# Sliding-window attention with sink tokens, then a gated feed-forward block: one sink table built later, sink scores of two groups in one run, crossbar transposes issued at earlier places

## The chip, the cores and the metric

The kernel runs on one core of a Trainium2 chip. Five engines work side by side on a core: TensorE (PE in the profile, with its weight loads as PEld), VectorE (DVE), ScalarE (ACT), GpSimd (POOL) and SyncE (SP), the last used here only to start DMAs. They synchronise through semaphores. TensorE reads SBUF and writes PSUM; PSUM has eight banks, and this kernel hands all of them out from one pool. The metric is device microseconds of one execution; lower is better.

## The reference, cut to what matters

```python
def _attn_ref(q, k, v, n_sink, window):          # batch 4, heads 8, seq 768, head_dim 64
    scores = (1 / sqrt(D)) * q @ k.T
    keep = (pos_k < 4) | ((0 <= pos_q - pos_k) & (pos_q - pos_k < 128))
    scores = where(keep, scores, -1e9)
    a = softmax(scores)
    return a @ v

x = attn_out.transpose(0, 2, 1, 3).reshape(3072, 512)
def _moe_ref(x, w_gate, w_val, w_out):           # 512 -> 1536 -> 512
    g = x @ w_gate
    return (g * sigmoid(g) * (x @ w_val)) @ w_out
```

Each query sees the four sink keys and the 128 keys of its window. The maximum is not subtracted in the kernel, and a column of ones beside V gives the sum of each row.

## The kernel before, in words

**Groups.** The 3072 tokens are cut into 12 groups of 256 tokens, three to a batch: group `g` is part `c = g % 3` of batch `b = g // 3`. A group passes these steps, each with its own function:

- Load (`load4`, `load1`, `load_v`, and `next_load(g)`, which loads group `g+4`): keys, queries and values by DMAs that POOL starts. The keys and queries of a group lie in a tile `kq` (four buffers).
- Transposition of keys and queries: groups 0 to 3 on TensorE (`step_T`, tile `pt`, copied to `kT` and `qT` by ACT and DVE); groups 4 to 11 by the DMA crossbar (`cross_T`, line 304, tile `kqT`, four buffers), two DMAs that SP starts. `C(g)` is `cross_T(g)` followed by `next_load(g)`; for `g` of 8 and above there is nothing left to load.
- `step_S(g, p2)`: window scores of four heads into four PSUM banks (line 334), the exponential by ACT (`e`, line 341), and a multiplication by the band mask by DVE (line 346), which is put on a list `later`.
- `step_K(g)`: sink scores of the group against the four sink keys of its batch, four matmuls into a bank `pk` (line 357) and the exponential `es` by ACT (line 361). Groups with `c == 0` need none, because for them the window mask takes in the sinks.
- `step_PV(g, j, hh)`: for 128 queries and four heads, probabilities times values into a bank `o` (line 381); the first matmul takes `es` and the sink value table `vsb` of the batch. DVE (`rcp` line 386, `xn` line 393; ACT in a few places, line 389) normalises. `vsb` (128 x 520) is made by POOL from a small fp32 table `vcf` and a diagonal pattern (`build_vsb`, line 188), once per batch.
- The normalised rows are transposed once more into `xT`: on TensorE (`step_X`, line 417) for groups 0 to 2 and 4, by the DMA crossbar from SP (line 399) for group 3 and from group 5 on.

**Feed-forward.** The tokens of `xT` are taken in eight blocks of 256, 256, 256, 512, 512, 512, 512 and 256. For a block, `gate(tb, f, attn)` computes a bank of the gate projection `pg` (line 445), lets ACT take its tanh (`th`, line 452), runs the attention steps of its slot, computes the value projection `pv` (line 445), and lets DVE form the product in two instructions (`u` line 459, `ht` line 460); then it empties `later`. `down(tb, ts, attn)` multiplies by `w_out` (`pd`, line 498), ACT copies (`ot`, line 502), and SP starts the store (line 504). The gate and value weights come in five chunks of two, two, two, two and four columns of 128 (`load_gate(0)` to `load_gate(4)`), by POOL's DMAs.

**The order is written by hand.** There is no scheduler: each engine executes what the Python code emits, in that order. `weave(units, slots)` runs through a list of `gate` and `down` calls and emits in each the attention steps of that slot. In a `gate`, they stand between `pg` and `pv`. There is a prologue (groups 0 and 1 up to the first scores), a first weave of 25 units (blocks 0 to 2 beside groups 1 to 4), three weaves of 16 units (block 3 with groups 5 and 6, block 4 with 7 and 8, block 5 with 9 and 10), and a last one (blocks 6 and 7 with group 11). The function `pair(ga, gb, sh)` gives the slots of two groups; `sh` shifts them. A sink-score run stands by itself in the second score slot of its group:

```python
        return [((s, s + 2), Ss(ga)), (s + 2, [K(ga)]),
                ...
                ((s + 6, s + 8), Ss(gb)), (s + 8, [K(gb)]),
```

**Queues.** The DMA queues of SP and POOL work in order as well: a DMA that waits holds up those behind it. Each starter's DMAs take eight semaphores in turn, so one also waits until the DMA eight places earlier has landed. A PSUM bank is handed out in the order in which earlier tiles were given back, so a step more or less shifts which earlier tile a later step waits for. In the prologue, POOL's order is: values of group 0, group 1, weight chunk 0, the two patterns for the table, values of group 1, chunk 1, `build_vsb(0)`, chunks 2 to 4.

Of the kernel before, what the change touches and what calls it, by code (L numbers as in the profile page):

```python
# [8 lines left out]
FP32 = mybir.dt.float32  # L9
BF16 = mybir.dt.bfloat16  # L10
AF = mybir.ActivationFunctionType
# [4 lines left out]
def kernel(  # L16
# [12 lines left out]
    nc = tc.nc  # L29
    P = 128  # L30
# [9 lines left out]
    NP2 = H // 2  # L40
# [12 lines left out]
    scale = 1.0 / float(D) ** 0.5  # L53

    def pool(name, bufs, psum=False):
        if psum:
            return ctx.enter_context(
                tc.tile_pool(name=name, bufs=bufs, space=bass.MemoryType.PSUM))
        return ctx.enter_context(tc.tile_pool(name=name, bufs=bufs))
# [8 lines left out]
    espool = pool("espool", 2)  # L68
# [11 lines left out]
    def bank(shape, dtype, name):  # L80
        return psum.tile(shape, dtype, tag="b", name=name)
# [36 lines left out]
    def load_v(g):  # L118
        va = new_v(g)
        b, c = divmod(g, GC)  # L120
        for j in range(2):
            t0 = c * 256 + j * P
            nc.gpsimd.dma_start(  # L123
                va[:, j, :, 0:D], v[b, :, t0:t0 + P].rearrange("h m d -> m h d"))
# [3 lines left out]
    def load_gate(i):  # L128
        f0, n = sum(FCH[:i]) * P, FCH[i] * P
        for lst, w, nm in ((wgs, moe_w_gate, "wg"), (wvs, moe_w_val, "wv")):  # L130
            t = wpool.tile([P, DMC, n], BF16, tag=f"{nm}{i}", name=nm)
            nc.gpsimd.dma_start(
                t, w[:, f0:f0 + n].rearrange("(c p) f -> p c f", p=P))
            lst.append(t)
# [17 lines left out]
    vsbs, kss = [], []  # L152
    KS = 32
# [32 lines left out]
    def build_vsb(b):  # L186
        vsb = const.tile([P, H, D + 1], BF16, tag=f"vsb{b}", name="vsb")
        nc.gpsimd.tensor_tensor(
            vsb,
            vcf[:, b:b + 1].broadcast_to([P, H, D + 1]),  # L190
            diag_h.rearrange("q (h o) -> q h o", o=1).broadcast_to([P, H, D + 1]),
            op=ALU.mult)
        vsbs.append(vsb)
# [19 lines left out]
        pattern=[[32, NP2], [NS, 2]], channel_multiplier=-1)  # L213
    load_v(1)
    load_gate(1)
    build_vsb(0)
    for i in range(2, 5):
        load_gate(i)

    def build_masks():  # L220
# [12 lines left out]
    kTs, qTs, es_t, e_t, xns, xTs = {}, {}, {}, {}, {}, {}  # L233
    later = []

    def A(fn, *a):
        return lambda: fn(*a)
# [12 lines left out]
    def step_T(g, ph, q_late=False, q_act=False):  # L250

        if ph == 0:
            new_kq(g)
        own = lambda i, p: nat[g][:, 2 * p:2 * p + 2]
        transpose(g, ph, own, (ident, ident), q_late, q_act)
# [36 lines left out]
    def queries(g, r, p, j, n):  # L292

        if g < NPE:
            return qTs[g][r, p, j * P:(j + n) * P]
        return cross[g][r, j:j + n, 1, p]
# [3 lines left out]
    def cross_T(g):  # L300

        t = crossp.tile([P, 2, 2, NP2, P], BF16, tag="kqT", name="kqT")
        for j in range(2):
            nc.sync.dma_start(
                t[:, j].rearrange("q i a m -> q (i a) m"),
                nat[g][:, j].rearrange("p i x -> p (i x)"), transpose=True)
        cross[g] = t
# [40 lines left out]
            later.append(dve)  # L348

    def step_K(g):  # L350
        b, c = divmod(g, GC)
        if c == 0:
            return
        ps = bank([P, 256], FP32, "pk")
        for p in range(NP2):

            nc.tensor.matmul(
                ps[KS * p:KS * (p + 1)], kss[b][:, p * KS:(p + 1) * KS],
                queries(g, slice(0, P), p, 0, 2), start=True, stop=True)
        es_t[g] = espool.tile([P, 256], BF16, tag="es", name="es")  # L360
        nc.scalar.activation(es_t[g], ps, AF.Exp, scale=scale)  # L361

    def step_PV(g, j, hh, act=False):
        b, c = divmod(g, GC)
# [146 lines left out]
    def gates(tb):  # L511
        return [(gate, tb, f) for f in range(0, DFC, 512 // SIZES[tb])]

    def downs(tb):
        return [(down, tb, t) for t in range(SIZES[tb] // P)]

    def next_load(g):
        if g + 4 < NG:
            (load4 if g + 4 < NPE else load1)(g + 4)
            load_v(g + 4)  # L520

    def sinks(b):
        return [lambda: later.append(A(step_ks, b))]

    def T(g):
        def last():
            step_T(g, 1)
            next_load(g)
        return [A(step_T, g, 0), last]

    def Ss(g):
        return [A(step_S, g, p2) for p2 in range(2)]

    def PVs(g):

        return [A(step_PV, g, j, hh) for hh in range(2) for j in range(2)]
# [4 lines left out]
    def K(g):  # L541
        return A(step_K, g)
# [5 lines left out]
    def weave(us, slots):  # L548
        assert all(i < len(us) for i in slots)
        for i, (fn, tb, x) in enumerate(us):  # L550
            fn(tb, x, slots.get(i, []))
# [7 lines left out]
    def slots(*pairs):  # L559
        sl = {}  # L560
        for at, steps in pairs:
            for i, step in zip(at if isinstance(at, tuple) else (at,) * len(steps),
                               steps):
                sl.setdefault(i, []).append(step)
        return sl

    def C(g):

        def last():
            cross_T(g)  # L570
            next_load(g)
        return [last]
# [41 lines left out]
    def first_PVs():  # L614
# [10 lines left out]
    weave(us, slots(  # L625
        (0, [flush, A(step_S, 1, 1), K(1), A(next_load, 1)]), (2, [first_PVs]),
        (3, [A(step_X, 1, 0), A(step_X, 1, 1, True), flush]),
        (9, T(2)), ((10, 11), Ss(2)), (11, [K(2)]),
        (12, PVs(2)[:2] + [flush]), (13, PVs(2)[2:] + [flush]), (13, C(4)),
        (14, [A(step_X, 2, 0), A(step_X, 2, 1, True), flush]),  # L630
        (15, T(3)), ((16, 17), Ss(3)), (17, sinks(1)), ((18, 18, 19, 19), PVs(3)),
# [2 lines left out]

    def pair(ga, gb, sh=0):
        s = sh
        return [((s, s + 2), Ss(ga)), (s + 2, [K(ga)]),
                ((s + 4, s + 5, s + 6, s + 7), PVs(ga)),
                ((s + 6, s + 8), Ss(gb)), (s + 8, [K(gb)]),
                ((11, 11, 12, 12) if s else (10, 11, 12, 13), PVs(gb))]  # L640

    weave(gates(3) + downs(3), slots(
        *pair(5, 6, 2), (2, C(6)), (10, C(7))))
    weave(gates(4) + downs(4), slots((0, sinks(2)), *pair(7, 8), (3, C(8)), (10, C(9)), (14, C(10))))
    weave(gates(5) + downs(5), slots((0, sinks(3)), *pair(9, 10), (10, C(11))))
    weave(gates(6) + gates(7) + downs(6) + downs(7), slots(
        ((0, 2), Ss(11)), (2, [K(11)]), ((4, 5, 6, 7), PVs(11))))


# [33 lines left out]
```

## Time and profile before

| | us |
|---|---|
| median of 6 runs | 245.44 (245.07 to 246.27) |
| the profiled execution, its own time | 245.09 |
| its span, first to last instruction | 243.4 |
| PE busy in the span | 233.9 (96%) |
| DVE busy | 160.5 (66%) |
| ACT busy | 111.3 (46%) |
| POOL busy | 71.1 (29%) |
| mean granted TensorE clock | 0.991 |

Instructions of one engine follow each other in time, and their durations can overlap at the ends, because the next one starts while the last one drains. A number in square brackets at the end of a row of the timeline is the idle time of the engine ahead of that row, with the instruction that ended it. The row of granted clock gives tenths of the full TensorE clock in 40 equal slices of the span, some 6.1 us each. TensorE is the engine with the least idle time, so the places where it stands still, and those where its clock is lowered, are what is read first.

### The profile page before, as it was taken

Reading aid. Unit: us, or ns where it says so; the run is one execution under the profiler, and the core shown is the slowest. Engines: PE = TensorE matmul, PEld = TensorE weight load, DVE = VectorE, ACT = ScalarE, POOL = GpSimd, SP = SyncE. Lnnn points to the kernel's source line nnn. Section 1 sums busy time; section 2 is a strip of 40 time slices with the busy share of each in tenths; the row PEclk is TensorE's granted clock in tenths of the full one; section 3 lists DMA queues with packets and bytes.
Section 4 is the critical chain, followed back from the end, with each engine's and each line's share of the span. In section 5 each row is a group of like instructions: output and inputs, shape, how many; then the busy total and the mean of one; then the engine's idle time right before and its main releaser. Section 6 shows DMA issues by size and latency. Waiting matters only on the chain.

```text
span 243.4 us, 5190 instructions
## 1 busy us (share of the span) xinstructions
PE 233.9 (96%) x2073; PEld 136.2 (56%) x2073; DVE 160.5 (66%) x336; ACT 111.3 (46%) x221; POOL 71.1 (29%) x92
## 2 busy tenths in 40 slices
PE   7779999999999999999999999999999999999994
PEld 2567887767755445554455454445454445488443
DVE  2688778929983489890598980399970489877100
ACT  2628627447461274532566512556612562232111
POOL 8995396794276714308000000000000000000000
PEclk9979999999999999999999999999999999999999
DMA  7999999999999999959940335900524200200132
GB/s 138 151 179 197 204 190 204 165 151 172 164 146 162 206 179 116 133 109 136 221 77 1 72 61 142 164 0 1 81 51 129 89 0 0 46 0 3 46 126 88
DMA packets 98792, 27.37 MB, mean 112 GB/s; under 512 B 84816, under 2 KB 95824, under 8 KB 98768
## 3 DMA queue, kind: packets, MB, share of 16 engines
q0 software_dynamic: 68832, 13.90, 69.8%
q1 hardware_dynamic: 29504, 12.75, 26.0%
q10 hardware_dynamic: 432, 0.39, 0.5%
q8 instruction: 16, 0.26, 0.5%
q14 instruction: 8, 0.07, 0.1%
HBM read 28.34 MB, written 6.29 MB: 142 GB/s over the span
## 4 chain that ended last, share of the span: by engine, by line
PE 87%; ACT 5%; DVE 5%; DMA 1%; issue 1%; DVEq 0%; ACTq 0%
PE pv L445 25%; PE pd L498 25%; PE pg L445 23%; PE o L381 5%; PE s L334 3%; ACT e L341 3%; PE pt L270 3%; DVE e L346 2%; PE wm L248 2%; DVE ht L460 1%; PE px L417 1%; DMA out_dram<-ot 1%; ACT xn L389 1%; DVE u L459 1%; ACT kT L275 0%
## 5 line engine op out<-in xcount | busy, mean ns | idle before, releaser
L445 PE MATMUL pv<-xT,wv 128*128 128x256 bf16 (+1 forms) x384 | 74.3, 326 | 0.9 <-DVE ht L460 0.9
L445 PE MATMUL pg<-xT,wg 128*128 128x256 bf16 (+1 forms) x384 | 74.2, 326 | 0.0
L452 ACT ACTIVATE th<-pg 128x512 f32<-128x512 f32 x72 | 43.7, 606 | 60.0 <-PE pg L445 59.4
L459 DVE SCALAR_TENSOR_TENSOR u<-th,pg 128x512 bf16<-128x512 f32 x72 | 49.2, 683 | 30.6 <-ACT th L452 30.1
L498 PE MATMUL pd<-wo,ht 128*128 128x512 bf16 x276 | 63.5, 379 | 0.0
L460 DVE TENSOR_TENSOR ht<-u,pv 128x512 bf16<-128x512 bf16 x72 | 49.5, 688 | 9.5 <-PE pv L445 2.9
L445 PEld LDWEIGHTS <-wg 128*128 128x128 bf16 x384 | 37.4, 98 | 25.4 <-issue 0.2
L341 ACT ACTIVATE e<-s 128x512 bf16<-128x512 f32 (+1 forms) x96 | 46.1, 580 | 0.9 <-PE s L334 0.8
L445 PEld LDWEIGHTS <-wv 128*128 128x128 bf16 x384 | 34.5, 98 | 21.0 <-issue 2.9
L498 PEld LDWEIGHTS <-ht 128*128 128x128 bf16 x276 | 25.8, 98 | 28.0 <-issue 0.2
L502 ACT ACTIVATE ot<-pd 128x512 f32<-128x512 f32 x23 | 13.7, 597 | 53.5 <-PE pd L498 53.5
L346 DVE TENSOR_TENSOR e<-e,mask 128x1024 bf16<-128x1024 bf16 (+1 forms) x48 | 30.4, 671 | 1.2 <-ACT e L341 1.0
L123 POOL DMA_DIRECT2D va<-in_v_dram x24 | 21.3, 896 | 5.8 <-DMA kq<-in_q_dram 2.0
L393 DVE TENSOR_TENSOR xn<-o,rcp 128x256 bf16<-128x256 f32 x46 | 19.5, 425 | 2.9 <-DMA xT<-xn 1.3
L107 POOL DMA_DIRECT2D kq<-in_k_dram x16 | 14.2, 889 | 24.1 <-DMA kqT<-kq 19.8
L381 PEld LDWEIGHTS <-e 128*128 128x128 bf16 x352 | 16.6, 99 | 7.9 <-DVE e L346 2.5
L381 PE MATMUL o<-va,e 128*128 128x65 bf16 x352 | 18.2, 195 | 2.1 <-DVE e L346 2.1
L107 POOL DMA_DIRECT2D kq<-in_q_dram x16 | 14.2, 890 | 7.1 <-DMA va<-in_v_dram 2.6
L386 DVE RECIPROCAL rcp<-o 128x4 f32<-128x4 f32 x48 | 8.4, 176 | 7.2 <-PE o L381 7.1
L275 DVE CAST qT<-pt 128x512 bf16<-128x512 f32 x7 | 4.6, 688 | 9.3 <-PE pt L270 9.3
L483 DVE TENSOR_SCALAR ot<-pd 128x256 f32<-128x256 f32 x1 | 0.4, 425 | 14.4 <-DMA out_dram<-ot 14.4
L381 PE MATMUL o<-vsb,es 128*128 128x260 bf16 x32 | 8.8, 275 | 0.7 <-ACT es L361 0.7
(61 smaller groups left out, 109.2 us busy)
## 6 DMA issues: line engine op xcount, KB each, us to landing
out_dram<-ot SPq DMA_DIRECT2D x23, 256.0 KB
va<-in_v_dram POOLq DMA_DIRECT2D x24, 128.0 KB, 9.1
kq<-in_k_dram POOLq DMA_DIRECT2D x18, 128.0 KB, 8.9
kq<-in_q_dram POOLq DMA_DIRECT2D x16, 128.0 KB, 9.1
wo<-in_moe_w_out_dram POOLq DMA_DIRECT2D x4, 384.0 KB, 12.8
wg<-in_moe_w_gate_dram POOLq DMA_DIRECT2D x4, 256.0 KB, 7.8
wv<-in_moe_w_val_dram POOLq DMA_DIRECT2D x4, 256.0 KB, 8.5
kq<-in_k_dram POOLq DMA_DIRECT2D x3, 256.0 KB, 9.6
```

Source lines behind the costliest of these rows:

```text
L107: nc.gpsimd.dma_start(x[:, j, i].rearrange("p (h d) -> p h d", d=D), src[b, :, t0:t0 + P].rearrange("h m d -> m h d"))
L123: nc.gpsimd.dma_start(va[:, j, :, 0:D], v[b, :, t0:t0 + P].rearrange("h m d -> m h d"))
L341: nc.scalar.activation(e_t[g][:, h0 + h, lo:512], pss[2 * pp + h][:, lo:512], AF.Exp, scale=scale)
L346: nc.vector.tensor_tensor(e, e, m[:, :, lo:512].broadcast_to([P, 2, 512 - lo]), op=ALU.mult)
L381: nc.tensor.matmul(o, l, r, start=(i == 0), stop=(i == len(mms) - 1), skip_group_check=True)
L393: nc.vector.tensor_tensor(xns[g, j][:, 256 * hh:256 * (hh + 1)].rearrange("p (h d) -> p h d", h=4), po[:, :, 0:D], rcp.broadcast_to([P, 4, ...
L445: nc.tensor.matmul(ps[:, i * n:(i + 1) * n], ws[fi][:, c, fo * P:(fo + 1) * P], x[:, 0:n // P, c], start=(c == 0), stop=(c == DMC - 1))
L452: nc.scalar.activation(th, pg, AF.Tanh, scale=0.5)
L459: nc.vector.scalar_tensor_tensor(u, th, 1.0, pg, op0=ALU.add, op1=ALU.mult)
L460: nc.vector.tensor_tensor(hts[tb][:, f:f + two].rearrange("p a n -> p (a n)"), u, pv, op=ALU.mult)
L498: nc.tensor.matmul(po, hts[tb][:, f, ts * P:(ts + 1) * P], wos[f // n][:, f % n], start=(f == 0), stop=(f == DFC - 1))
L502: nc.scalar.activation(ot, po, AF.Copy, scale=0.5)
```

## The change

Three things are changed; the arithmetic is the same.

1. In the prologue, `build_vsb(0)` moves behind the loads of weight chunk 2 on POOL.
2. `step_K` can take two groups in one run: for batches 2 and 3 the sink scores of parts 1 and 2 go into the two halves of one bank, and one ACT instruction (128 x 512 in place of two of 128 x 256) takes their exponential. The calls for groups 8 and 11 go. The others stand at new places: `K(2)` in slot 10 of the first weave (was 11), `K(5)` ahead of the scores of its group in slot 2 (was behind, in slot 4), `K(7)` for groups 7 and 8 in slot 2, `K(10)` for groups 10 and 11 in slot 6 of its weave (was 8).
3. The crossbar work is emitted sooner: `C(7)` in slot 6 of the weave of block 3 (was 10), `C(8)` in slot 9 of that weave (was slot 3 of the next), `C(9)`, `C(10)` and `C(11)` in slots 3, 7 and 10 of the weave of block 4 (were slots 10 and 14 of that weave and slot 10 of the next).

```diff
     load_gate(1)
+    load_gate(2)
     build_vsb(0)
-    for i in range(2, 5):
+    for i in range(3, 5):
         load_gate(i)
...
     def step_K(g):
         b, c = divmod(g, GC)
-        if c == 0:
-            return
-        ps = bank([P, 256], FP32, "pk")
-        for p in range(NP2):
-            nc.tensor.matmul(
-                ps[KS * p:KS * (p + 1)], kss[b][:, p * KS:(p + 1) * KS],
-                queries(g, slice(0, P), p, 0, 2), start=True, stop=True)
-        es_t[g] = espool.tile([P, 256], BF16, tag="es", name="es")
-        nc.scalar.activation(es_t[g], ps, AF.Exp, scale=scale)
+        n = 2 if b > 1 else 1
+        assert n == 1 or c == 1
+        ps = bank([P, n, 256], FP32, "pk")
+        for i in range(n):
+            for p in range(NP2):
+                nc.tensor.matmul(
+                    ps[KS * p:KS * (p + 1), i], kss[b][:, p * KS:(p + 1) * KS],
+                    queries(g + i, slice(0, P), p, 0, 2), start=True, stop=True)
+        es = espool.tile([P, 2, 256], BF16, tag="es", name="es")
+        nc.scalar.activation(es[:, 0:n], ps, AF.Exp, scale=scale)
+        for i in range(n):
+            es_t[g + i] = es[:, i]
...
-        (9, T(2)), ((10, 11), Ss(2)), (11, [K(2)]),
+        (9, T(2)), ((10, 11), Ss(2)), (10, [K(2)]),
...
-        return [((s, s + 2), Ss(ga)), (s + 2, [K(ga)]),
-                ((s + 4, s + 5, s + 6, s + 7), PVs(ga)),
-                ((s + 6, s + 8), Ss(gb)), (s + 8, [K(gb)]),
+        return [((s, s + 2), Ss(ga)), ((s + 4, s + 5, s + 6, s + 7), PVs(ga)),
+                ((s + 6, s + 8), Ss(gb)),
                 ((11, 11, 12, 12) if s else (10, 11, 12, 13), PVs(gb))]
     weave(gates(3) + downs(3), slots(
-        *pair(5, 6, 2), (2, C(6)), (10, C(7))))
-    weave(gates(4) + downs(4), slots((0, sinks(2)), *pair(7, 8), (3, C(8)), (10, C(9)), (14, C(10))))
-    weave(gates(5) + downs(5), slots((0, sinks(3)), *pair(9, 10), (10, C(11))))
+        (2, [K(5)]), *pair(5, 6, 2), (2, C(6)), (6, C(7)), (9, C(8))))
+    weave(gates(4) + downs(4), slots(
+        (0, sinks(2)), *pair(7, 8), (2, [K(7)]), (3, C(9)), (7, C(10)), (10, C(11))))
+    weave(gates(5) + downs(5), slots(
+        (0, sinks(3)), *pair(9, 10), (6, [K(10)])))
     weave(gates(6) + gates(7) + downs(6) + downs(7), slots(
-        ((0, 2), Ss(11)), (2, [K(11)]), ((4, 5, 6, 7), PVs(11))))
+        ((0, 2), Ss(11)), ((4, 5, 6, 7), PVs(11))))
```

## The prediction, made before the changed kernel was run

> **What bounds the kernel now.** I read first the busy shares and the granted clock, then the waits of TensorE, then the timeline around each of them.
>
> ```profile
> PE 233.9 (96%) x2073; PEld 136.2 (56%) x2073; DVE 160.5 (66%) x336; ACT 111.3 (46%) x221; POOL 71.1 (29%) x92
> PEclk9979999999999999999999999999999999999999
> ```
>
> TensorE is the bound. It is idle for 243.4 - 233.9 = 9.5 us, and its clock is low in one place after the start, the third slice. A change can gain there, or by less TensorE work. The waits (total, times, longest):
>
> ```profile
> PE o L381 <- DVE e L346: 2.1, 3, 1.1
> PE pv L445 <- DVE ht L460: 0.9, 3, 0.4
> PE o L381 <- ACT es L361: 0.7, 2, 0.4
> ```
>
> The first is the prologue. Rows of the timeline (start, us, engine, instruction) of DVE, POOL and TensorE:
>
> ```profile
> 9.83 0.56 DVE L346 TENSOR_TENSOR e<-e,mask 128x768 bf16<-128x768 bf16 x1
> 10.60 0.56 DVE L346 TENSOR_TENSOR e<-e,mask 128x768 bf16<-128x768 bf16 x1 [0.21 <-ACT e L341]
> 11.36 1.12 DVE L346 TENSOR_TENSOR e<-e,mask 128x768 bf16<-128x768 bf16 x1 [0.21 <-ACT e L341]
> 12.41 1.41 DVE L346 TENSOR_TENSOR e<-e,mask 128x768 bf16<-128x768 bf16 x1
> ...
> 12.12 1.29 POOL L188 TENSOR_TENSOR vsb<-vcf,diag_h 128x520 bf16<-128x520 f32 x1
> ...
> 13.88 0.73 PE L381 MATMUL o<-va,e 128*128 128x65 bf16 x10 [1.10 <-DVE e L346]
> ```
>
> Four equal mask multiplications: two take 0.56 us, the two that overlap POOL's table build take 1.12 and 1.41, and TensorE stands still for the last one. The clock follows (columns: PE, PEld, DVE, ACT, POOL busy, clock):
>
> ```profile
> 10.49:13.90 3.41, 1.26 (x17) 0.69 (x16) 3.09 (x4) 1.61 (x5) 3.41 (x5) 1.00 1.35 173
> 13.90:17.32 3.42, 3.42 (x82) 2.96 (x82) 2.83 (x10) 1.07 (x2) 3.25 (x5) 0.50 1.93 175
> ```
>
> After 3.4 us in which TensorE was busy for only 1.26, it runs 3.4 us at half clock. The chain of waits shows that this stretch sets the end:
>
> ```profile
> 13.88 0.73 PE o L381 x10
> 14.61 1.00 PE pt L270 x30
> 15.61 0.97 PE px L417 x8
> 16.58 1.00 PE pt L270 x32
> 17.57 0.57 ACT kT L275
> ```
>
> The three later places where the sink scores stand in the way:
>
> ```profile
> 45.00 0.28 PE L381 MATMUL o<-vsb,es 128*128 128x260 bf16 x1 [0.35 <-ACT es L361]
> ...
> 135.59 0.29 PE L357 MATMUL pk<-kqT,ks 128*32 128x256 bf16 x4
> 136.09 1.02 PE L445 MATMUL pv<-xT,wv 128*128 128x512 bf16 x4 [0.21 <-DVE ht L460]
> ...
> 171.70 0.29 PE L357 MATMUL pk<-kqT,ks 128*32 128x256 bf16 x4
> 172.31 1.02 PE L445 MATMUL pv<-xT,wv 128*128 128x512 bf16 x4 [0.32 <-DVE ht L460]
> ```
>
> **Part 1, the table behind chunk 2.** POOL ends the issue of chunk 1 at 12.14. Two issues of chunk 2 follow (0.81 and 0.76 in the rows at 13.36 and 14.16), and the table starts at about 13.7. Each issue also waits until the DMA eight places earlier has landed: keys and queries of group 1, issued at 5.32 and 6.00, 6.1 and 6.7 us to landing, hence 11.4 and 12.7: in time for 12.12 and 12.9. From chunk 3 on POOL's order is as before. The table is read first at 22.90, so 15.0 in place of 13.4 costs nothing.
>
> Masks: they start 0.77 apart (9.83, 10.60, 11.36), so the fourth can start at 12.13 and, at 0.56, end at 12.69 in place of 13.82: 1.13 earlier. The third is stretched although the table's row begins only at 12.12, when it should have been done (11.92). POOL's spans are rough, but if something else stretches it, the gain is 0.85 (12.41 + 0.56 = 12.97). Descriptor work is no candidate: the first two ran beside DMA issues (9.76, 10.62) at 0.56.
>
> [...]
>
> What is late next is DVE's normalisation, four pairs of `rcp` and `xn`. The last ended at 16.02, 2.20 after the mask; that becomes 14.89. The table now lies beside these (13.7 to 15.0). Bounds: nothing, by `u` and `ht` of 0.69 beside the builds at 31.43 to 34.53, whose other rows are 0.69 too; or up to the 1.41 that both masks lost. I take nothing: `u`, `ht` and `xn` each have one input in PSUM, both mask inputs are in SBUF.
>
> After the last `xn` come four `px` and 32 `pt`: 17.57 - 16.02 = 1.55 at half clock. At full clock, four `px` take 0.23 (50.54 to 50.77) and 32 `pt` 0.51 (half of the 1.02 for 64 at 36.76), with 0.05 to start 0.79. So ACT's copy at 17.57 comes 1.13 earlier at half clock, 1.13 + 0.76 = 1.89 at full clock. Which? In the 3.41 us to 13.90, TensorE would be busy 1.26 plus about 0.9 of scores and transposes, 63%. The stretch before (7.08 to 10.49) had 2.65, 78%, and kept the clock; 37% lost it. 63% is nearer to 78%: full clock, and 1.1 stays an end.
>
> [...]
>
> Cover for the 1.89: chunk 1 lands at 10.62 + 7.8 = 18.4 and 11.36 + 8.4 = 19.8; TensorE would want it at 18.7 and 19.6. The 0.2 lies under the wait for ACT's `es` (22.90, now 21.0). Queries of group 2 land at 20.07 + 14.1 = 34.2; wanted at 36.69 - 1.89 = 34.8, a margin of 0.6. From there to 100 us the DMA engines are full, and loads keep their own times.
>
> **Part 2, the sink scores.** `K(2)` sooner: ACT's `es` is done before the scores of slot 11. The first `o` waited until 45.00, `pg` before it started at 43.62 and takes 0.87 in a row: 44.49 is possible, gain 0.51. Late next is ACT: `th` of slot 11 moves from 42.07 to 42.5, `u` from 43.00 to 43.1, the last mask from 45.71 to 45.84, wanted at 46.5: covered.
>
> Slots 8 of the weaves of blocks 4 and 5: `pk` takes 0.23, then `pv` waits for a bank. Without `pk` in the slot, `pv` takes the bank that `pk` took, freed by `u` (134.56 + 0.68 = 135.24) and not by the `ht` after it (136.04). It starts at 135.59, 0.50 earlier; in block 5 likewise 0.61. The four matmuls of `K(8)` and `K(11)` are done elsewhere, behind four others: 0.11 more (256 columns, as in `pv` 128x256, 0.87 for 8) to 0.23 (a run alone). Block 4: 0.50 - 0.23 + (0.23 - 0.11 to 0.23) = 0.27 to 0.39. Block 5: 0.61 - 0.23 = 0.38 to 0.50; the pair in slot 6 needs a bank that `ht` frees at 167.02 and `pv` one that `xn` frees at 167.56, and they want them at 167.35 and 167.7: covered, barely. ACT: one instruction of 0.61 for two of 0.44, off the path; behind it in slot 6 `th` ends at 170.4, before DVE asks for it at 170.79. The pairs need `kqT` of groups 8 and 11 sooner, at 122 and 167; they are issued at about 102 and 139. `K(5)` ahead of its scores: same work, `kqT` landed by 79.6 (its load buffer was reused then). I take 0.51 + 0.3 + 0.4 = 1.2, with ends 0 and 1.4.
>
> **Part 3, crossbar work.** SP does not wait for slots, only for its queue and for data. Transposes of group 7 follow those of group 6 at 87.8 (82.08 + 5.69) in place of 105.14, group 8 comes at 102, groups 9 to 11 at 118, 134 and 139. With `C(7)` goes the last load, group 11: six issues of 0.89, last in POOL's queue, from 110.18 to about 100. Behind the moved pairs on SP wait `xT` of groups 5, 7 and 8, 2.6 us for a pair (105.14, 137.98); wanted at 116.67 and 153.91, due at 104.8, 138 and 148. Off the path: nothing, between the bounds of the slow rival and zero.
>
> **The sum.** 1.89 + 1.2 = 3.1. The profiled execution took 245.09 (span 243.4, 1.7 around it): 242.0. The median lies 0.35 above that execution: 242.4 for the median after.
>
> **The rivals.** (a) The half clock stays: 1.13 + 1.2, 242.8 by the execution, 243.1 by the median. For it: 63% is untested. (b) The masks stay stretched, because the table is not the cause: 1.2 alone, 243.9 to 244.2. Against it: the two stretched rows are the two that touch the build. (c) The gain is given back to loads that keep their own times, at 34.2 and later: under 0.7 in all. Against it: the margins above. (d) Slower: the pair of group 7, now issued while the DMA engines are full, holds up the pair of group 6 in front of it. That one landed by 94.52 (POOL's wait) and is wanted by the scores at 98.19 - 3 = 95.2. If it is pushed back by the time of a pair, up to 7.83 in SP's rows, TensorE waits to 102.4, 7.2 us: 245.4 - 3.0 + 7.2 = 249.6. It turns the sign from a landing after 98.9 on. Against it: the queue serves the pair in front first.
>
> **How the numbers follow.** A measurement of this kernel tells 0.3%, 0.74 us, from no change. Forecast 0.50, (a) 0.27, (b) 0.09, (c) 0.06, (d) 0.08. The first three are faster by more: 0.86. Range: below, 1.4 in part 2 and 0.35 of spread, 241.7; above, to the end of (b), 244.2. Left out are (c) and (d), 0.14.
>
> **What would show it.** Right: all four masks at 0.56; no 1.10 wait ahead of `o`; no 0.50 clock after the start-up; `es` and both `ht` waits gone, the one of 0.41 at 66.75 still there, some 2.4 to 3 us earlier; scores of group 6 without a wait. Wrong: a mask over 1 us, `xn` over 0.43 beside the table, a wait for a DMA ahead of `pt` or `s`.

## The result, and the profile after

| | us |
|---|---|
| median before | 244.99 (72 runs, 243.14 to 246.44) |
| median after | 244.67 (35 runs, 243.71 to 246.67) |
| ratio after / before | 0.9996, 95% interval 0.9982 to 1.0009 |
| span of the profiled execution, before and after | 243.4, 242.9 |

No change that this measurement can tell. The forecast was 3.1 us less (242.4, from the median of 245.44 that six runs gave; 72 runs give 244.99), so the question is where they went. The page after has the same shape as the page before, TensorE busy a little less and the low clock still in the third slice:

```profile
PE 233.0 (96%) x2073; PEld 135.0 (56%) x2073; DVE 159.2 (66%) x336; ACT 110.9 (46%) x219; POOL 70.7 (29%) x92
PEclk9979999999999999999999999999999999999999
```

The waits of TensorE after the change (total, times, longest). Both waits for `es` and two of the three for `ht` are gone, as forecast. At the top stands a wait that the kernel before does not have; "issue" means that the profile names no releaser. The 0.8 us of `pt` lies at 7.04, at the keys of group 0 and ahead of everything that was changed:

```profile
PE pg L450 <- issue: 1.7, 1, 1.7
PE o L386 <- DVE e L347: 1.4, 3, 0.5
PE pt L271 <- DMA kq<-in_k_dram: 0.8, 1, 0.8
PE pv L450 <- DVE ht L465: 0.4, 1, 0.4
```

The start-up, in rows of the timeline of DVE and POOL. The four masks are equal now, and the table (last row) is built behind them:

```profile
9.62 0.56 DVE L347 TENSOR_TENSOR e<-e,mask 128x768 bf16<-128x768 bf16 x1 [0.66 <-ACT e L342]
10.39 0.56 DVE L347 TENSOR_TENSOR e<-e,mask 128x768 bf16<-128x768 bf16 x1 [0.21 <-ACT e L342]
11.15 0.56 DVE L347 TENSOR_TENSOR e<-e,mask 128x768 bf16<-128x768 bf16 x1 [0.21 <-ACT e L342]
11.92 0.56 DVE L347 TENSOR_TENSOR e<-e,mask 128x768 bf16<-128x768 bf16 x1 [0.21 <-ACT e L342]
...
13.47 1.13 POOL L188 TENSOR_TENSOR vsb<-vcf,diag_h 128x520 bf16<-128x520 f32 x1
```

From the first mask to the end of the fourth it is 12.48 - 9.62 = 2.86 us, before it was 13.82 - 9.83 = 3.99: the 1.13 of the forecast, to the hundredth. The clock did not follow (columns as before: PE, PEld, DVE, ACT, POOL busy, clock):

```profile
7.78:11.20 3.42, 2.70 (x48) 1.47 (x41) 2.31 (x7) 2.98 (x8) 3.33 (x6) 1.00 1.46 173
11.20:14.61 3.41, 2.18 (x60) 1.45 (x56) 3.07 (x11) 1.67 (x4) 3.41 (x6) 1.00 1.62 182
14.61:18.02 3.41, 3.29 (x51) 2.30 (x52) 2.17 (x10) 1.95 (x5) 2.92 (x4) 0.50 1.75 184
```

TensorE was busy for 2.18 of 3.41 us, 64%, and the next 3.4 us ran at half clock all the same. These stretches begin at 7.78 and 11.20 here, and at 7.08 and 10.49 before: they do not start with the program.

Where the rest went is read by laying the two chains of waits side by side and comparing the start of the same piece of work. Before:

```profile
36.76 1.02 PE pt L270 x64
...
98.70 0.97 PE pv L445 x4
...
119.22 0.86 PE pg L445 x4
...
224.44 12.96 PE pd L498 x60
```

After:

```profile
35.72 1.02 PE pt L271 x64
...
97.14 0.97 PE pv L450 x4
...
99.45 7.94 DMA xT<-xn
...
108.53 7.48 DMA xT<-xn
116.01 1.00 issue
117.01 1.02 PE pg L450 x4
...
119.55 0.86 PE pg L450 x4
...
223.91 12.96 PE pd L503 x60
```

TensorE is 1.04 us ahead at the transposes of group 2, 1.56 at 98.70, 0.33 behind at the second `pg` of block 4, and 0.53 ahead at the last projection. So 1.89 us are lost in one place, the start of block 4, whose first `pg` waits for the normalised rows that the crossbar transposes, and 0.86 are won after it. That the page names no releaser ("issue") hides a DMA: the last of the four pieces of `xT` landed at 116.81, and `pg` began 0.20 later, at 117.01. In `after_no_table` below, where the profile does name the DMA, it is 0.20 too (117.31 and 117.51).

The slots where `pk` stood in the way, after the change; `pv` follows the scores with no wait ahead of it:

```profile
135.49 0.61 PE L335 MATMUL s<-kqT 64*128 64x128 bf16 x12
136.04 1.04 PE L450 MATMUL pv<-xT,wv 128*128 128x512 bf16 x4
...
171.45 0.62 PE L335 MATMUL s<-kqT 64*128 64x128 bf16 x12
171.99 1.04 PE L450 MATMUL pv<-xT,wv 128*128 128x512 bf16 x4
```

### The profile page after: what moved, and what is told of

It is laid out like the page before. It is cut to its first block, busy times and chain, and to the rows that moved or that the text cites. A ratio compares the mean times of both kernels' runs of the same rounds, so it can differ in the third digit from the quotient of the medians.

```text
span 242.9 us, 5187 instructions
## 1 busy us (share of the span) xinstructions
PE 233.0 (96%) x2073; PEld 135.0 (56%) x2073; DVE 159.2 (66%) x336; ACT 110.9 (46%) x219; POOL 70.7 (29%) x92
## 4 chain that ended last, share of the span: by engine, by line
PE 83%; DMA 9%; ACT 2%; DVE 2%; issue 1%; POOL 0%; POOLq 0%; ACTq 0%; DVEq 0%
PE pv L450 26%; PE pg L450 25%; PE pd L503 20%; DMA xT<-xn 6%; PE o L386 5%; PE s L335 5%; DMA kq<-in_k_dram 2%; PE pt L271 2%; ACT e L342 1%; DVE xn L398 1%; DMA out_dram<-ot 1%; ACT xn L394 1%; PE pk L360 1%; PE px L422 1%; DVE rcp L391 0%
## 5 line engine op out<-in xcount | busy, mean ns | idle before, releaser
L347 DVE TENSOR_TENSOR e<-e,mask 128x1024 bf16<-128x1024 bf16 (+1 forms) x48 | 29.1, 642 | 2.1 <-ACT e L342 1.9
L335 PE MATMUL s<-kqT 64*128 64x128 bf16 (+1 forms) x168 | 9.4, 238 | 0.0
(61 smaller groups left out, 104.8 us busy)
## 6 DMA issues: line engine op xcount, KB each, us to landing
wo<-in_moe_w_out_dram POOLq DMA_DIRECT2D x4, 384.0 KB, 12.8
```

The lines of the kernel that those rows point to most:

```text
L335: nc.tensor.matmul(pss[2 * pp + h][:, col:col + n * P], keys(b, t, r, p), queries(g, r, p, j, n), start=True, stop=True)
L347: nc.vector.tensor_tensor(e, e, m[:, :, lo:512].broadcast_to([P, 2, 512 - lo]), op=ALU.mult)
```

## The experiments

SP's queue is what the experiments turn on. A group's keys and queries are one pair of crossbar transposes, its normalised rows two more. I call each DMA a piece, 5a, 5b, 6a and 6b the four pieces of rows that block 4 waits for. In the kernel before, SP issued 5a, 5b, pair 7, 6a, 6b; in the changed one pair 7, 5a, pair 8, 5b, 6a, 6b, and the load of group 11, which needs the buffer that pair 7 frees, is issued from 99.24 in place of 110.18, beside all of them. Landings are the last completion of each DMA in the trace; "wanted" is when TensorE is done with what stands ahead of the first `pg` of block 4. Behind "Measured" stand the median, that of the kernel before in the same round where it is given, and the ratio of the two kernels with its 95% interval; the ratio need not be that of the medians.

| kernel | pair 8 ahead of 5b | load of group 11 | 5a | 5b | 6a | 6b | wanted |
|---|---|---|---|---|---|---|---|
| before | no | late | 104.30 | 106.24 | 111.62 | 115.11 | 116.83 |
| changed | yes | early | 107.39 | 114.30 | 116.01 | 116.81 | 115.28 |
| `c8_behind` | no | early | 107.43 | 110.36 | 113.51 | 114.00 | 115.52 |
| `both_late` | no | late | 103.33 | 104.02 | 109.40 | 113.35 | 114.6 |
| `c8_then_c7` | yes, and pair 7 ahead of 6a | from 107 on | 104.13 | 107.17 | 115.50 | 117.23 | 115.51 |
| `no_load11` | yes | none | 105.85 | 108.89 | 109.61 | 110.90 | 114.8 |

The first piece, 5a, needs a remark. In the five traces in which SP issues pair 7 ahead of it, it took 6.9 to 7.9 us from issue to landing, and in the six others 3.0 to 4.6. The kernel without the load of group 11 is among the five (98.99 to 105.85), so the delay of 5a is for the most part not that load's. `c8_behind` and `both_late` differ in the place of `C(7)` alone: 7.74 against 4.55. With pair 7 in front, the load of group 10 landed later too: issued from 93.2 on in `no_load11` and from 93.3 in `both_late`, its last DMA landed at 106.92 and 102.75. What the load of group 11 and the pair of group 8 do shows behind 5a, from there to 6b.

### The table alone

The kernel before with one part of the change:

```diff
     load_gate(1)
+    load_gate(2)
     build_vsb(0)
-    for i in range(2, 5):
+    for i in range(3, 5):
         load_gate(i)
```

> The kernel before with the first sink table behind chunk 2 and nothing else. In the trace of the changed kernel TensorE is 1.04 us ahead at the transposes of group 2 (35.72 against 36.76), and gives everything back at 117.01, where the first gate projection of block 4 waits for the transposed rows of group 6 (landed 116.81). Queue theory: that landing was late because of the crossbar pairs and the load that were moved in front of it; without the moves it lands at 115.1 or sooner, wanted at 116.83 - 1.04 = 115.79, so the whole 1.04 stays: about 244.0 us, ratio 0.996. Floor theory: these rows land at 115 to 117 whatever comes before, since the loads keep the DMA engines full: 0.0 to 0.7 us, ratio 0.997 to 1.000. Both: all four masks of 0.56 us; the half-clock stretch of 3.4 us may shift but stays.

Measured: 243.63 against 244.98, ratio 0.9949 (0.9930 to 0.9968). The first `pg` of block 4 starts 1.43 us sooner than before (115.40 against 116.83) and the end is 1.46 us sooner by the span: what the start-up brings (1.43 here, 1.04 in the trace of the changed kernel) stays, to the end. 6b landed at 113.80. The queue theory holds, the floor theory falls.

### The table and the place of `K(2)`, nothing moved on SP

```diff
-        (9, T(2)), ((10, 11), Ss(2)), (11, [K(2)]),
+        (9, T(2)), ((10, 11), Ss(2)), (10, [K(2)]),
```

> The kernel before with the table behind chunk 2 and the sink scores of group 2 in slot 10; no merged sink scores, no moved crossbar work. TensorE should be 1.04 + 0.52 = 1.56 us ahead at 100 us, as in the changed kernel. Queue theory: the rows of group 6 land by 115.1 or sooner and are wanted at 115.27: all 1.56 stay, about 243.4 us, ratio 0.9936. Floor theory: they land at 116 or later: 0.6 us at most, ratio 0.9975 or more.

Measured: 243.30, ratio 0.9945 (0.9920 to 0.9970). In the trace TensorE is 1.69 us ahead of before at block 4 (115.14 against 116.83), no wait there (6b landed at 113.26), and 1.7 at the end. Between blocks 1 and 2 it gains 0.52: `K(2)`, as in the changed kernel. (`K(5)` was left where it was.)

### The pair of group 8 behind the rows

The changed kernel with one number changed:

```diff
-        (2, [K(5)]), *pair(5, 6, 2), (2, C(6)), (6, C(7)), (9, C(8))))
+        (2, [K(5)]), *pair(5, 6, 2), (2, C(6)), (6, C(7)), (12, C(8))))
```

> The changed kernel with the crossbar pair of group 8 in slot 12 (was 9) of the weave of block 3, which puts it behind the rows of groups 5 and 6 on SP; the load of group 11 still starts early. Queue theory, pair in front: in the changed kernel the pair of group 8 took from 107.39 to 112.88; without it the rows of group 6 land at about 111.4, wanted at 115.27: 1.56 + 0.23 (block 4) + 0.48 (blocks 5 and 6) = 2.27 us less than before, ratio 0.991. Load theory: the early load of group 11, which competes until 117.6, is what slows the rows; they land at 115 or later and 0.5 to 1.7 of the 2.27 is lost. Floor theory: nothing gained, ratio 0.999.

Measured: 242.43 against 244.98, ratio 0.9904 (0.9874 to 0.9935): 2.4 us less, with a change of one slot. SP now issues the four pieces in a row, with the pair behind them (rows of the timeline of SP):

```profile
99.69 11.33 SPq L404 DMA_TRANSPOSE xT<-xn  x4
111.12 3.10 SPq L305 DMA_TRANSPOSE kqT<-kq  x2
```

and block 4 starts without a wait (timeline of TensorE):

```profile
113.63 1.89 PE L503 MATMUL pd<-wo,ht 128*128 128x512 bf16 x8
115.36 1.03 PE L450 MATMUL pg<-xT,wg 128*128 128x512 bf16 x4
```

The rows landed at 114.00, later than the 111.4 of "pair in front" and sooner than the 115 of the load theory: with the load early and the pair of group 8 behind them the rows are in time. That 5a still lands at 107.43 is not due to that pair and, as said above, for the most part not to the load.

### Both moved back

```diff
-        (2, [K(5)]), *pair(5, 6, 2), (2, C(6)), (6, C(7)), (9, C(8))))
+        (2, [K(5)]), *pair(5, 6, 2), (2, C(6)), (10, C(7)), (12, C(8))))
```

> The changed kernel with the crossbar pair of group 7 and the load of group 11 behind it back in slot 10, and that of group 8 in slot 12: on SP the order of before, with the pair of group 8 ahead of four stores. Queue and load theory: the rows of group 6 land as before, 115.1 or up to 1.5 sooner, wanted at 115.27: the 1.56 stays, with 0.23 in block 4 and 0.48 in blocks 5 and 6 it is 2.0 to 2.3 us, ratio 0.991 to 0.992. Floor theory: landing 116 or later, at most 1.3 us, ratio 0.995 or more.

Measured: 242.42, ratio 0.9906 (0.9879 to 0.9933). No different from `c8_behind`, although the rows land 0.65 us sooner: once they are in time, more of it brings nothing. The pair of group 8 lands late here, at 120.42, and the `pk` that reads it takes 0.70 in place of 0.40 us. In this trace the clock never dropped in the start-up (1.00 in every stretch up to 23.60).

### Without the table

The changed kernel with `build_vsb(0)` back ahead of `load_gate(2)`.

> The changed kernel with the first sink table in its old place, ahead of chunk 2: only the sink scores and the crossbar work are changed. Queue theory: the rows of group 6 land when the SP queue lets them, near 116.8, and not when TensorE is done with them; so what the table brings before that is lost anyway, and without it block 4 starts at about 117 too: within 0.4 us of the changed kernel, ratio 0.998 to 1.002 against before. Additive theory: the table is worth its 1.0 to 1.4 us here as it is alone, so the time is 245.7 to 246.1, ratio 1.003 to 1.005.

Measured: 244.90, ratio 1.0005 (0.9979 to 1.0030); the changed kernel has 0.9996. The part that is worth 0.5% alone is worth 0.1% here, where the rows of group 6 are late, and the intervals do not tell that from nothing. The masks are stretched again (two in one row of DVE), and block 4 starts at 117.51 after a wait that the profile names this time:

```profile
10.88 2.79 DVE L346 TENSOR_TENSOR e<-e,mask 128x768 bf16<-128x768 bf16 x2 [0.21 <-ACT e L341]
...
117.51 1.02 PE L449 MATMUL pg<-xT,wg 128*128 128x512 bf16 x4 [1.40 <-DMA xT<-xn]
```

### Pairs in front, load behind them

```diff
-        (2, [K(5)]), *pair(5, 6, 2), (2, C(6)), (6, C(7)), (9, C(8))))
+        (2, [K(5)]), *pair(5, 6, 2), (2, C(6)), (9, C(8)), (10, C(7))))
```

> The changed kernel with the pair of group 7, and the load of group 11 that follows it, back in slot 10, while the pair of group 8 stays in slot 9: both pairs now stand in front of the rows of group 6 on SP, but the load of group 11 starts only after them. Theory that the pairs in front are enough: two pairs and three halves at 1.2 to 3 us each behind 102 put the landing at 116 or later: ratio 0.996 to 1.000. Theory that it takes the early load too (in the changed kernel the first half of the rows of group 5 needed 7.9 us beside it): the pairs move at the rate of before, 1.1 to 2.1 us a piece, the rows of group 6 land by 115.3: ratio 0.990 to 0.993.

Measured: 244.32, ratio 0.9980 (0.9957 to 1.0002), inside the range of the first expectation. The trace agrees: 6b landed at 117.23, and

```profile
117.43 1.02 PE L450 MATMUL pg<-xT,wg 128*128 128x512 bf16 x4 [1.92 <-issue]
```

By itself it does not separate the pairs from the load, since the load did not wait for pair 7 as I had expected: with the calls exchanged it takes the buffer that pair 8 frees, and POOL issues it from 107.16. Up to there SP's pieces land 0.6 to 1.4 us apart (104.13, 105.17, 106.59, 107.17), behind it 2.0, 3.6, 2.8 and 1.7. Beside `both_late` it says more: there the load starts at nearly the same time (107.92), the pair of group 8 stands behind the rows, and 6b lands at 113.35, 3.88 us sooner.

### No load at all

```diff
     def next_load(g):
-        if g + 4 < NG:
+        if g + 4 == NG - 1:
+            nat[g + 4], vas[g + 4] = nat[g + 3], vas[g + 3]
+        elif g + 4 < NG:
```

> The changed kernel without the six loads of group 11; its steps read the tiles of group 10 instead. Both crossbar pairs stay where the change put them, in front of the rows of groups 5 and 6. So far: with load and pair in front the rows of group 6 landed at 116.8 (changed kernel) and 117.2 (pair of group 7 behind that of group 8), with the load alone at 114.0. Theory that it takes the load and the pair: without the load a piece takes 1.0 to 1.4 us, as it did in front of the load in the kernel with the pairs exchanged, the rows land by 111 or as soon as TensorE and VectorE have made them, wanted at about 115.3: 1.0 to 1.7 from the start-up, 0.52, 0.38 and 0.48: ratio 0.988 to 0.992. Theory that the pair in front is enough: the rows land at 115.5 or later, ratio 0.995 or more.

The kernel leaves out the six loads of group 11, and the steps of that group read the tiles of group 10, so what it computes for those 256 tokens is not what the reference asks for. Measured: 242.28 against 244.78, ratio 0.9898 (0.9864 to 0.9932). SP's order is that of the changed kernel, and the rows land at 110.90. From 5a to 6b there are five pieces: 110.90 - 105.85 = 5.05 us here, 116.81 - 107.39 = 9.42 in the changed kernel. So neither of the two alone makes the rows late (114.00 with the load and without the pair ahead, 110.90 with the pair and without the load); together they do.

### Matmuls in the waits of the start-up

The kernel before, with warm-up matmuls of unused result put into two waits:

```diff
-    warm(2)
+    wps = warm(2)
...
-    step_PV(0, 0, 1)
+    fill(wps, 3)
+    step_PV(0, 0, 1, fills=(wps, 4))
...
```

`fill(wps, 3)` emits three of them; with `fills`, `step_PV` emits four behind its second matmul.

> The kernel before with seven matmuls of the warm-up kind (0.21 us each, their result unused) in two waits for the mask, three ahead of the third and four inside the last pair of probabilities times values. Nothing else moves, the masks stay stretched. Clock theory: a stretch of 3.41 us in which TensorE is busy for less than about two thirds is followed by one at half clock; with 1.5 us more the stretch stays above that, no half clock after the start-up, 0.5 to 0.8 us less, ratio 0.997 to 0.998. Theory that the clock drop costs nothing beside the waits: ratio 1.000.

Measured: 244.29 against 245.10, ratio 0.9975 (0.9951 to 0.9999). In the trace the masks are stretched as before, the stretch around the waits is busy for 2.93 of 3.41 us, 86%, and the next one keeps its clock:

```profile
11.21:14.62 3.41, 2.93 (x58) 1.45 (x55) 3.34 (x7) 0.58 (x2) 3.40 (x5) 1.00 1.54 181
14.62:18.03 3.41, 2.88 (x64) 1.98 (x60) 2.98 (x13) 2.40 (x5) 2.54 (x4) 1.00 1.80 182
```

TensorE is 0.85 us ahead from there to the end. All 12 timed executions kept the full clock (mean 0.997 to 1.000). The clock alone has a price, 0.85 us in this trace, near the 0.76 that the prediction gave it.

### Everything together

`c8_behind` with two, one, two and one such matmuls in the waits for the masks and ahead of `step_X(0, 0)`.

> The changed kernel with the pair of group 8 in slot 12, and six such matmuls in the waits for the masks and for the normalised rows of group 0 (two, one, two and one). Clock theory: no half clock after the start-up wherever the 3.41 us stretches fall; 0.3 to 0.9 us less than the same kernel without them (242.43): 241.5 to 242.1, ratio 0.986 to 0.989. Other theory: the time goes into the loads of group 1, wanted at 13 us, and the matmuls bring nothing: 242.4, ratio 0.990.

Measured: 242.08 against 245.10, ratio 0.9888 (0.9860 to 0.9916). The timed step from `c8_behind` is within the intervals; the traces show it. The page:

```profile
PE 232.1 (97%) x2065; PEld 134.2 (56%) x2079; DVE 159.0 (66%) x336; ACT 110.9 (46%) x219; POOL 70.8 (29%) x92
PEclk9999999999999999999999999999999999999999
```

No half clock after the start-up, span 240.3. TensorE is ahead of before by 1.77 at the transposes of group 2, 2.29 at block 4, 2.66 at block 5 and 3.15 at block 7. This is the sum that was forecast, 3.1, in the kernel that has no late rows and no low clock; its median is the lowest here, and all six timed executions kept the full clock (1.000).

## Why the prediction was wrong

**The masks (1.13): right.** 2.86 us for four in place of 3.99. All three traces with the table in its old place stretch the last two masks (1.12 and 1.41 before; 2.79 and 2.49 for the two in `after_no_table` and `before_fill`), none of the others does. The third mask is stretched although POOL's row begins after its normal end (12.12 against 11.92), so that rival (b) falls, and the 0.85 with it. `xn` beside the table kept 0.42, as assumed; that its input in PSUM is the reason was not tested. `before` and `table_only` differ by the place of the table alone (third and fourth mask 1.12 and 1.41 against 0.56 and 0.56), so the cause is shown, though not how the table stretches a mask. One cover was not costed: group 1's keys and queries, which TensorE now wants at 12.8 to 13.1. In `c8_behind` it waited 1.02 us for the queries, and its start-up gained only 0.80.

**The clock (0.76): the size of the step was right, the choice was wrong.** "63% is nearer to 78%: full clock." The share was 64%, and the clock fell. In the profiled execution rival (a), at 0.27, had this right. Two things were missing. First, the stretches were taken to begin where they did in the one profile (7.08, 10.49). In the seven traces with the table behind chunk 2 and no added matmuls they begin elsewhere each time, the first boundary after 6 us at 6.54 to 8.99 in place of 7.08; in two of them the clock stayed (`both_late`, `no_load11`: gain 1.75 and 1.73 at block 1), in five it fell (0.80 to 1.43). Second, the limit lies between the two shares that the prediction compared. `both_late`, which kept its clock, and `c8_then_c7`, which lost it:

```profile
9.95:13.36 3.41, 2.24 (x51) 1.43 (x49) 2.72 (x8) 2.13 (x6) 3.41 (x5) 1.00 1.40 186
13.36:16.78 3.42, 2.90 (x89) 2.06 (x78) 3.10 (x10) 2.04 (x4) 3.10 (x5) 1.00 1.93 175
```

```profile
11.74:15.15 3.41, 2.23 (x60) 1.51 (x64) 3.02 (x12) 1.32 (x3) 2.86 (x4) 1.00 1.68 173
15.15:18.56 3.41, 3.41 (x52) 2.30 (x49) 2.26 (x8) 2.48 (x5) 2.21 (x3) 0.50 1.65 188
```

Once the clock was up, all stretches of 2.23 us and less in the start-up of the eleven traces were followed by half clock, all of 2.24 and more by full clock: near two thirds, by a busy time that is itself modelled. This limit holds for the start-up alone. At the wait of block 4 TensorE was busy for 1.68 us (49%) of the stretch from 113.60 in the changed kernel and for 1.49 (44%) of the one from 114.14 in `c8_then_c7`, and both were followed by full clock. The matmuls there have 512 columns, those of the stretch that lost the clock in the changed kernel (11.20 to 14.61) at most 128; whether that is the reason was not tested, so a share of busy time alone does not tell when the clock falls.

**The sink scores (1.2): right.** `K(2)` 0.52, forecast 0.51. Block 4 gains 2.66 - 2.29 = 0.37 in `c8_fill` (0.27 to 0.39), blocks 5 and 6 another 3.15 - 2.66 = 0.49 (0.38 to 0.50), and the changed kernel has the same: 0.33 behind at block 4, 0.53 ahead at the end. The sum is 1.38, within the ends. (The lower end of the whole range, 241.7, comes out at 241.8 from the terms that it names: 245.44 - 1.89 - 1.4 - 0.35.)

**The crossbar work ("off the path: nothing"): wrong, and this is the step that failed.** It cost 1.89 us and undid most of the rest. The paragraph named the rows of groups 5, 7 and 8 as what waits behind the moved pairs, and left out those of group 6, which come next on the same queue, although the trace of before had them: landed 115.11, wanted 116.83. A margin of 1.72 had to bear a gain of 2.4 ahead of it and two added pieces in front; in the changed kernel they landed at 116.81, wanted at 115.28. The second error is the price: "2.6 us for a pair" came from rows of SP in which no POOL load was under way, and the same edit puts the load of group 11 beside it. Rows of group 5 "due at 104.8" landed at 107.39 and 114.30. From 5a to 6b the five pieces took 9.42 us beside the load and 5.05 without; 5a itself was late without the load too (105.85), behind pair 7.

The runs show that SP's pieces stretch beside POOL's load (five of them 9.42 us against 5.05); by what mechanism, they do not show.

**The rivals.** (c), the gain given back to transfers, at 0.06 and "under 0.7 in all", was the right kind: it named loads that keep their own times, and the late transfer was one that the change itself had made late. (d) had the right kind of cause, moved pairs among full DMA engines (the row DMA of the changed kernel's page is 9, 90% and more, from 6 to 121 us) that delay another transfer, at the wrong transfer: it held the pair of group 6 back behind that of group 7, but that one landed at 93.09 (before: 93.97), and what was held back were the rows behind.

## What to carry to other kernels

When transfers are issued sooner on a queue whose transfers land in the order of issue, as SP's did (107.39, 112.88 for the end of pair 8, 114.30, 116.01, 116.81 in the changed kernel), list every transfer that now stands behind them up to the next one with slack, with its landing and the time at which it is wanted after the gains ahead of it, and take its duration from rows with the same company. The gain ahead of the late transfer was lost whole here (1.56 us ahead at 98.70, 0.33 behind in block 4), so look for the smallest margin downstream: it capped the sum, and parts worth 1.04 and 0.52 showed nothing in the time of the changed kernel until one call moved by three slots. Where the clock falls after a thinly busy stretch, as it did here after 2.18 of 3.41 us, fill the waits rather than count on where the stretch begins: all 18 timed executions of the two kernels with added matmuls kept the full clock (mean 0.997 to 1.000).

## What the runs showed that was not expected

The transposing DMAs of SP land 0.55 to 1.3 us apart when no load of POOL is under way (`no_load11` behind 107.45) and one took 7.9 us from issue to landing beside the loads of groups 10 and 11 (5a in the changed kernel, 99.45 to 107.39). The 3.41 us stretches of the clock begin at a different point in each of the eleven traces (the first boundary after 6 us lies from 6.54 to 8.99), and 0.01 us of modelled busy time separated the stretch that kept the clock (2.24) from the one that lost it (2.23).

The mean clock on record for each timed execution shows how much of the spread goes with this. One such stretch at half clock in 243 us makes a mean of 0.993, two make 0.986. For the 63 executions of the kernel before that were run beside the experiments, and the 35 of the changed kernel:

| mean granted clock | kernel before, executions | median, us | changed kernel, executions | median, us |
|---|---|---|---|---|
| 0.997 and more | 8 | 243.37 | 15 | 244.41 |
| 0.990 to 0.993 | 35 | 244.84 | 15 | 244.67 |
| 0.984 to 0.986 | 20 | 245.44 | 5 | 246.18 |

So the changed kernel keeps its clock more often, and where both keep it, it is the slower of the two; its late rows would explain that, but no such execution of either kernel was profiled. The clock is not all that sets the full-clock executions of the kernel before apart: `before_fill`, which always keeps it, has a median of 244.29, and `table_only` with full clock (5 executions) 243.51, no less than the kernel before with full clock. What else differs in those executions, the masks perhaps, stays open.
